# Turning by transposing transfers out of SBUF instead of on TensorE and through DRAM

## The chip, the cores and the metric

One core of one Trainium2 chip. The metric is the device time of one execution in microseconds (us). A profiled execution has a span, the time between its first and last instruction, and its own time, which is a little longer. Engine names are those of the profile: PE is TensorE's matmul, PEld its weight load, DVE VectorE, ACT ScalarE, POOL GpSimd, SP SyncE; SPq is SP's queue, on which nearly all transfers of this kernel are issued in order.

## What is computed

S = 2048 rows of D = 512 in bf16. A layer norm gives xn; a local attention (32 heads of 16, 8 keys at steps of 2 positions) and a mixing network both work on xn; the result is x + s * silu(g).

```python
def _B_ref(x, w1, w2, w3, w4):          # x is xn
    h = _gelu(_layernorm(x, axis=-1) @ w1)
    # g0..g3: the four quarters of h, moved along the rows by +1, -1, +2, -2
    hs = jnp.concatenate([g0, g1, g2, g3], axis=-1) @ w2
    x1 = x + hs
    h2 = _gelu(_layernorm(x1, axis=-1) @ w3) @ w4
    return x1 + h2

xn = _layernorm(A_x, axis=-1)
s = _A_ref(xn, A_wqkv, A_wo)            # q, k, v, softmax over 8 keys, @ wo
g = _silu(_B_ref(xn, B_w1, B_w2, B_w3, B_w4))
return A_x + s * g
```

w1 and w2 are 512x512, w3 is 512x1376, w4 1376x512, wqkv 512x1536.

## The kernel before

The rows are split by parity: p = 0 holds the even ones, p = 1 the odd ones, 1024 each. Each half is two chunks of 512 rows (chunk c has p = c // 2), each chunk four tiles of 128 rows. A tile of xn has rows on the partitions; a matmul that contracts over D needs D on the partitions, so each tile must be turned into "columns".

Every instruction that matters is pinned to the order in which the program emits it, engine by engine. So lines 505 to 599 are the order of the work, written out by hand: each engine, and SP's queue, takes its own instructions in this order. PE's sequence before the attention stage is: v, q and k of chunk 0, w1 of chunk 0, and then by chunk q, k, v, w1 with the turning work in between, then w2(0), q and k of chunk 3, w2(1), w2(2), w3(0), w2(3), w3(1) to w3(3). The attention stage (lines 878 to 936) follows from about 112 us; it mixes scores, softmax, values, w4 and the output projection.

What the steps below speak of:

- `Norm` (210 to 240): statistics and apply on DVE, the root on POOL (`rsqrt_eps`, 203). Layer norm l1 is applied in place on x (L237), l3 on x1 into a tile xn3.
- `turn` (296): 8 PE transposes (L302) of two tiles into PSUM and a DVE copy (L303) into xnT. It runs twice for each of chunks 1, 2 and 3; chunk 0 has `turn_one` and one `turn`.
- Row factors: the second norm in front of w1 works on rows that are normed already, so it is one factor for each row, `rows2` (248), made on POOL into r2b with rows on partitions. The product `scaled` (288, L291 on DVE) needs it along the free dimension on all partitions. `rows2_spread` (264, chunks 1 and 2) transposes r2b on PE (L266), copies it on DVE (L268), writes 4 rows of 128 to DRAM (L269) and reads them back broadcast to 128 partitions (L271). `rows2_here` (273, chunks 0 and 3) makes it with one DVE product (L277), one matmul with ones (L282) and a copy.
- `proj` (323) holds the matmuls of q, k and w1 (L328): 16 matmuls of 128x512 for a call with two output tiles, in a pair of PSUM banks. There are three such pairs, used in turn; ACT empties them (L339 q, L354 k, L400 w1's gelu).
- `w2` (415): 16 matmuls (L427), then on DVE the sum into x (L435), the statistics (L221), and the root on POOL.
- `columns` (443): the apply of l3, a write of the chunk to DRAM (L446), and a transposing transfer of 512x512 back into x1nT (L450), which `w3` (459, L469) reads.
- Loads on SP's queue: w3's is issued at line 545, behind the row factors of chunk 1; w4's at 574 and 578; `v_keep` (367, L377) writes v to DRAM.

Of the kernel before, what the change touches and what calls it, by code (L numbers as in the profile page):

```python
# [8 lines left out]
AF = mybir.ActivationFunctionType  # L9
ALU = mybir.AluOpType  # L10
BF16 = mybir.dt.bfloat16
# [9 lines left out]
def kernel(  # L21
# [17 lines left out]
    PE, DVE, ACT, POOL, SP = nc.tensor, nc.vector, nc.scalar, nc.gpsimd, nc.sync  # L39

    def pin(ins):

        return tc.keep_in_program_order(ins)

    P = 128
    S = 2048
    D = 512
    F = 1376
    ND = D // P
# [4 lines left out]
    CH = 512  # L54
    NCH = S // CH
    TPC = CH // P
# [22 lines left out]
    dram = ctx.enter_context(tc.tile_pool(name="dram", bufs=1, space=bass.MemoryType.DRAM))  # L79
# [16 lines left out]
    def single():  # L96
        cnt["s"] += 1
        return PS[:, 6 + (cnt["s"] - 1) % 2, :]


    xn = [b8([P, M // P, D], f"xn{p}") for p in range(2)]
# [24 lines left out]
    w3_sb = wpl.tile([P, WS], BF16, name="w3_sb", tag="w")[:, 0 : ND * F].rearrange("p (dt f) -> p dt f", f=F)  # L126
# [4 lines left out]
    ident = const.tile([P, P], BF16, name="ident")  # L131
# [61 lines left out]
    xnT = [b8([P, ND, M], f"xnT{p}") for p in range(2)]  # L193
# [2 lines left out]
    kM = [kbp.tile([P, ND, MK, 2], BF16, name=f"kM{p}", tag="kM") for p in range(2)]  # L196
    v_d = [dram.tile([MK, 2, D], BF16, name=f"v_d{p}") for p in range(2)]
    r2_d = dram.tile([NCH, CH], BF16, name="r2_d")
    x1n_dram = dram.tile([S, D], BF16, name="x1n_dram")
    vst = [b4([P, 2, 2, D], f"vst{i}") for i in range(2)]  # L200


# [4 lines left out]
    def small_t(name, shape, dt=F32):  # L207
        return small.tile(shape, dt, name=name, tag=name)
# [33 lines left out]
    def x_of(c):  # L242
        p, k = c // 2, c % 2
        return xn[p][:, k * TPC : (k + 1) * TPC, :]

    xn2Ts, r2s = {}, {}

    def rows2(c, ln):

        r2 = small_t("r2", [P, TPC])  # L250
        r2b = small_t("r2b", [P, TPC], BF16)
        eng = DVE if c == 0 else POOL
        pin(eng.tensor_tensor(out=r2, in0=ln.rstd, in1=ln.rstd, op=ALU.mult))
        pin(eng.tensor_tensor(out=r2, in0=r2, in1=ln.mv[:, :, 1], op=ALU.mult))
        if c == 0:
            pin(ACT.activation(r2, r2, AF.Sqrt, bias=eps_t[:]))
            with nc.allow_low_precision("bf16 row factors"):
                pin(DVE.reciprocal(out=r2b, in_=r2))
        else:
            rsqrt_eps(r2, r2)  # L260
            pin(POOL.tensor_copy(out=r2b, in_=r2))
        r2s[c] = r2b

    def rows2_spread(c):
        pt = single().bitcast(BF16)[0:TPC, 0:P]
        pin(PE.transpose(pt, r2s[c], ident[:]))  # L266
        t = small_t("r2t", [TPC, P], BF16)
        pin(DVE.tensor_copy(out=t, in_=pt))  # L268
        pin(SP.dma_start(out=r2_d[c].rearrange("(j q) -> j q", q=P), in_=t))  # L269
        xn2Ts[c] = b4([P, ND, CH], "xn2T")  # L270
        pin(SP.dma_start(out=xn2Ts[c][:, ND - 1, :], in_=r2_d[c : c + 1, :].to_broadcast([P, CH])))  # L271

    def rows2_here(c):

        xn2Ts[c] = t = b4([P, ND, CH], "xn2T")
        d = t[:, 0, :].rearrange("p (j q) -> p j q", q=P)
        pin(DVE.tensor_tensor(  # L277
            out=d, in0=ident.unsqueeze(1).to_broadcast([P, TPC, P]), in1=r2s[c].unsqueeze(2).to_broadcast([P, TPC, P]),
            op=ALU.mult,
        ))  # L280
        pt = single()
        pin(PE.matmul(pt, lhsT=ones_bf[:], rhs=t[:, 0, :], start=True, stop=True))  # L282
        if c == 0:
            pin(ACT.activation(t[:, ND - 1, :], pt, AF.Copy))
        else:
            pin(DVE.tensor_copy(out=t[:, ND - 1, :], in_=pt))

    def scaled(c):
        p, k = c // 2, c % 2
        t = xn2Ts[c]  # L290
        pin(DVE.tensor_tensor(  # L291
            out=t, in0=xnT[p][:, :, k * CH : (k + 1) * CH],
            in1=t[:, ND - 1, :].unsqueeze(1).to_broadcast([P, ND, CH]), op=ALU.mult,
        ))

    def turn(c, h):
        p, k = c // 2, c % 2
        i = k * TPC + 2 * h
        pt = single().bitcast(BF16).rearrange("p (a j q) -> p a j q", a=ND, j=2)
        for j in range(2):  # L300
            for dt in range(ND):
                pin(PE.transpose(pt[:, dt, j, :], xn[p][:, i + j, dt * P : (dt + 1) * P], ident[:]))  # L302
        pin(DVE.tensor_copy(  # L303
            out=xnT[p][:, :, i * P : (i + 2) * P], in_=pt.rearrange("p a j q -> p a (j q)")
        ))

    def turn_one(c, t):
        p, k = c // 2, c % 2
        i = k * TPC + t
        pt = single().bitcast(BF16)[:, 0 : ND * P].rearrange("p (a q) -> p a q", a=ND)  # L310
        for dt in range(ND):
            pin(PE.transpose(pt[:, dt, :], xn[p][:, i, dt * P : (dt + 1) * P], ident[:]))
        pin(ACT.activation(xnT[p][:, :, i * P : (i + 1) * P], pt, AF.Copy))

    def q_half(pts, lo, hi, nts=range(ND)):
        for nt in nts:
# [32 lines left out]
    def k_all(c, parts=(0, 1)):  # L349
        p, k = c // 2, c % 2  # L350
        for a in parts:
            pt = proj(c, a, wqk_sb[:, :, D : 2 * D], chunk(xnT, c))
            for e in range(2):
                pin(ACT.activation(  # L354
                    kM[p][:, 2 * a : 2 * a + 2, 8 + k * CH : 8 + (k + 1) * CH, e], pt, AF.Copy, scale=em[:, e : e + 1]
                ))
# [29 lines left out]
    def v_pair(p, t):  # L386
        pt = pair()
        for i in range(2):
            v_mm(p, t + i, pt[:, i, :])
        v_keep(p, t, 2, pt[:, 0, :])  # L390

    def v_pad(p):
        rows = v_d[p].rearrange("r e d -> (r e) d")
        pin(SP.dma_start(out=rows[0:16], in_=zero[0:16, :]))
        pin(SP.dma_start(out=rows[2 * (M + 8) : 2 * MK], in_=zero[0:4, :]))

    def w1(c, a):
        p, k = c // 2, c % 2
        pt = proj(c, a, w1_sb, xn2Ts[c])
        pin(ACT.activation(  # L400
            hT[p][:, 2 * a : 2 * a + 2, 1 + k * CH : 1 + (k + 1) * CH], pt, AF.Gelu_apprx_tanh
        ))
# [12 lines left out]
    def w2(c, order="a0 s0 a1 s1"):  # L415

        p, k = c // 2, c % 2
        x_c = x_of(c)
        ln = ln2[c] = Norm(x_c, b4([P, TPC, D], "xn3"), TPC, "l3")
        pts = []  # L420
        for h in range(TPC // 2):
            pt = pair()
            pts.append(pt)
            for j in range(2):
                m0 = k * CH + (2 * h + j) * P
                for g in range(ND):
                    pin(PE.matmul(  # L427
                        pt[:, j, :], lhsT=w2_src(p, g, m0), rhs=w2_sb[:, g, :],
                        start=(g == 0), stop=(g == ND - 1),
                    ))  # L430
        for what, i in (w for w in order.split()):
            if what == "a":
                h = int(i)
                xs = x_c[:, 2 * h : 2 * h + 2, :]
                pin(DVE.tensor_tensor(out=xs, in0=pts[h], in1=xs, op=ALU.add))  # L435
            elif what == "s":
                h = int(i)
                ln.stats(2 * h, 2 * h + 2)
            else:
                columns(c - 1)  # L440
        ln.root()

    def columns(c):
        ln = ln2[c]
        ln.apply(0, TPC)
        pin(SP.dma_start(  # L446
            out=x1n_dram[c * CH : (c + 1) * CH, :].rearrange("(i q) d -> q i d", q=P), in_=ln.dst
        ))
        x1nT = b4([P, ND, CH], "x1nT")
        pin(SP.dma_start_transpose(out=x1nT, in_=x1n_dram[c * CH : (c + 1) * CH, :]))  # L450
        x1nTs[c] = x1nT

    h3a, h3b = {}, {}
# [75 lines left out]
    for a in range(2):  # L529
# [10 lines left out]
    v_pair(0, 2)  # L540
    k_all(0, (1,))
    v_pad(0)
    w1(0, 0)
    rows2_spread(1)
    pin(SP.dma_start(out=w3_sb, in_=B_w3.rearrange("(dt q) f -> q dt f", q=P)))
    turn(1, 0)
    turn(1, 1)
    w1(0, 1)
    l2 = Norm(x_of(2), x_of(2), TPC, "l1")
    l2.stats(0, 4)  # L550
    l2.root()
    l2.apply(0, 4)
    rows2(2, l2)
    l3 = Norm(x_of(3), x_of(3), TPC, "l1")
    l3.stats(0, 4)
    l3.root()
    scaled(1)
    q_all(1)
    k_all(1)
    v_pair(0, 4)  # L560
    l3.apply(0, 4)
    rows2(3, l3)
    v_pair(0, 6)
    rows2_spread(2)
    w1(1, 0)
    turn(2, 0)
    turn(2, 1)
    w1(1, 1)
    scaled(2)
    q_all(2)  # L570
    turn(3, 0)
    turn(3, 1)
    k_all(2)
    pin(SP.dma_start(
        out=w4_sb[:, 0 : NF - 1, :],
        in_=B_w4[0 : (NF - 1) * P, :].rearrange("(ft q) n -> q ft n", q=P),
    ))
    pin(SP.dma_start(out=w4_sb[0:FL, NF - 1, :], in_=B_w4[(NF - 1) * P : F, :]))
    rows2_here(3)
    scaled(3)  # L580
    w1(2, 0)
    w1(2, 1)
    w1(3, 0)
    w1(3, 1)
    w2(0)
    columns(0)
    v_pad(1)
    q_all(3)
# [289 lines left out]
    for n in range(NU):  # L878
        now["n"] = n
        q = W4 * (n + 1) // NU - given  # L880
# [111 lines left out]
```

## Time and profile before

| | us |
|---|---|
| median of 3 runs | 197.82 (197.75 to 199.02) |
| profiled execution, own time | 197.26 |
| its span | 195.5 |
| PE busy | 185.5 |
| ACT busy | 133.3 |
| DVE busy | 117.8 |
| POOL busy | 19.1 |
| w2(0) begins on PE | 53.0 |
| w3(0) begins on PE | 70.8 |
| attention stage begins on PE | 112.2 |

The granted clock of TensorE was 0.996 of full speed. Busy times overlap: an engine that is busy for less than the span may still hold up another one at a single place, so what counts is which engine the others wait for at that place. A row of the time line is: start, length, engine, line of the kernel, operation, what it writes and reads, how many, and in brackets how long the engine was idle before and what ended that. For a transfer the row on SPq is its issue alone; the data land later.

### The profile page before, as it was taken

What the parts mean: (1) busy time and instruction counts of PE and PEld (TensorE: products, weight loads), DVE (VectorE), ACT (ScalarE), POOL (GpSimd) and SP (SyncE); (2) the same over time, 40 slices, a digit from 0 to 9 for tenths busy, and PEclk for the clock granted to TensorE, in tenths of its full rate; (3) what the DMA queues carried; (4) which work ended last, traced back from release to release, by engine and by line L of the source; (5) the groups of instructions that cost most, each with busy time, mean ns of one, the idle gap of its engine ahead of it and who ended that gap; (6) DMA issues with size and microseconds to landing.
All of it is one profiled execution on the core that took longest, in us unless ns stands there. A gap on an engine that the chain in (4) does not pass through costs nothing.

```text
span 195.5 us, 5255 instructions
## 1 busy us (share of the span) xinstructions
PE 185.5 (95%) x2253; PEld 91.8 (47%) x2283; DVE 117.8 (60%) x229; ACT 133.3 (68%) x151; POOL 19.1 (10%) x57
## 2 busy tenths in 40 slices
PE   7899999999999999999999999999999999999990
PEld 2474544554444444444444444445444544554540
DVE  5785767236076697494200035556487888798894
ACT  7399769649817615435656588877887876887871
POOL 3006066100002022006000000000000000000000
PEclk9999999999999999999999999999999999999998
DMA  4997480654000433752480051457565556582523
GB/s 131 339 368 239 132 282 15 218 158 157 0 0 3 136 83 109 215 107 65 110 260 0 0 162 60 157 166 232 153 216 161 137 155 215 127 247 51 171 91 126
DMA packets 33576, 28.12 MB, mean 144 GB/s; under 512 B 10760, under 2 KB 32528, under 8 KB 33552
## 3 DMA queue, kind: packets, MB, share of 16 engines
q1 hardware_dynamic: 33408, 27.71, 47.2%
q8 instruction: 18, 0.29, 0.6%
q10 hardware_dynamic: 144, 0.07, 0.1%
q14 instruction: 6, 0.05, 0.1%
HBM read 17.01 MB, written 8.67 MB: 131 GB/s over the span
## 4 chain that ended last, share of the span: by engine, by line
PE 85%; DMA 5%; DVE 4%; issue 2%; SPq 1%; ACT 1%
PE PS L469 19%; PE PS L328 19%; PE PS L764 19%; PE PS L427 5%; PE PS L811 4%; PE PS L795 4%; PE PS L652 3%; DMA wqk_sb<-in_A_wqkv_dram 3%; PE PS L626 3%; PE PS L362 3%; DMA x1nT<-x1n_dram 2%; PE PS L318 2%; PE PS L662 2%; PE PS L302 2%; DVE sg L825 2%
## 5 line engine op out<-in xcount | busy, mean ns | idle before, releaser
L469 PE MATMUL PS<-x1nT,w_sb 128*128 128x512 bf16 (+1 forms) x173 | 38.2, 379 | 0.4 <-DMA x1nT<-x1n_dram 0.3
L633 ACT ACTIVATE prob<-PS 128x1824 bf16<-128x1824 f32 x18 | 30.4, 1688 | 4.4 <-PE PS L626 3.6
L764 PE MATMUL PS<-w_sb,h3a 128*128 128x512 bf16 x112 | 29.2, 379 | 1.9 <-issue 1.7
L475 ACT ACTIVATE h3a<-PS 128x1024 bf16<-128x1024 f32 x16 | 16.4, 1024 | 21.0 <-PE PS L469 19.1
L777 DVE TENSOR_TENSOR xn<-PS,xn 128x512 bf16<-128x512 f32 x15 | 10.3, 686 | 32.0 <-PE PS L764 31.8
L469 PEld LDWEIGHTS <-w_sb 128*128 128x128 bf16 (+1 forms) x176 | 17.5, 100 | 20.9 <-issue 0.7
L328 PE MATMUL PS<-xnT,wqk_sb 128*128 128x512 bf16 x109 | 25.0, 379 | 0.2
L354 ACT ACTIVATE kM<-PS,em 128x1024 bf16<-128x1024 f32 x16 | 20.8, 1404 | 3.2 <-PE PS L328 3.2
L638 DVE TENSOR_TENSOR prob<-prob,maskb 128x1824 bf16<-128x1824 bf16 x18 | 19.8, 1102 | 1.8 <-ACT prob L633 1.8
L764 PEld LDWEIGHTS <-h3a 128*128 128x128 bf16 x128 | 11.3, 97 | 13.4 <-issue 1.2
L328 PEld LDWEIGHTS <-wqk_sb 128*128 128x128 bf16 x112 | 10.9, 98 | 12.8
L435 DVE TENSOR_TENSOR xn<-PS,xn 128x1024 bf16<-128x1024 f32 x8 | 9.6, 1213 | 11.3 <-PE PS L427 11.3
L811 PE MATMUL PS<-wo_sb,oT 128*128 128x512 bf16 (+1 forms) x68 | 15.5, 366 | 0.0
L328 PE MATMUL PS<-xn2T,w_sb 128*128 128x512 bf16 x62 | 14.6, 379 | 0.1
L427 PE MATMUL PS<-w_sb,hT 128*128 128x512 bf16 x63 | 14.4, 379 | 0.1
L821 ACT ACTIVATE sg<-PS 128x512 bf16<-128x512 f32 (+1 forms) x17 | 9.6, 572 | 6.1 <-PE PS L811 6.1
L764 PE MATMUL PS<-w_sb,h3b 128*128 128x512 bf16 (+1 forms) x44 | 12.8, 380 | 0.8 <-issue 0.8
L339 ACT ACTIVATE qT<-PS 128x1024 bf16<-128x1024 f32 x8 | 8.1, 1024 | 7.6 <-PE PS L328 7.6
L373 ACT ACTIVATE vst<-PS 128x512 bf16<-128x512 f32 (+1 forms) x12 | 8.8, 743 | 3.5 <-ACT sig L784 2.3
L221 DVE BATCH_NORM_STATS2 l1s<-xn 128x6 f32<-128x512 bf16 x16 | 10.1, 680 | 1.6 <-DMA xn<-in_A_x_dram 1.6
L400 ACT ACTIVATE hT<-PS 128x1024 bf16<-128x1024 f32 x8 | 8.1, 1031 | 3.8 <-PE PS L328 3.8
L221 DVE BATCH_NORM_STATS2 l3s<-xn 128x6 f32<-128x512 bf16 x16 | 10.2, 682 | 0.2
(105 smaller groups left out, 229.2 us busy)
## 6 DMA issues: line engine op xcount, KB each, us to landing
ring<-v_d SPq DMA_DIRECT2D x18, 256.0 KB, 3.3
v_d<-vst SPq DMA_DIRECT2D x16, 256.0 KB, 2.7
x1n_dram<-xn SPq DMA_DIRECT2D x4, 512.0 KB
xo<-in_A_x_dram SPq DMA_DIRECT2D x8, 256.0 KB, 4.1
ring<-rec_d SPq DMA_DIRECT2D x4, 456.0 KB, 4.7
out_dram<-xo SPq DMA_DIRECT2D x7, 256.0 KB
xn<-in_A_x_dram SPq DMA_DIRECT2D x6, 256.0 KB, 7.9
w_sb<-in_B_w_dram SPq DMA_DIRECT2D x1, 1376.0 KB
```

What stands on the lines that cost most here:

```text
L221: pin(DVE.bn_stats(out=self.st[:, j, :], in_=self.src[:, j, :]))
L328: pin(PE.matmul(pt[:, b, :], lhsT=w[:, dt, nt * P : (nt + 1) * P], rhs=rhs[:, dt, :], start=(dt == 0), stop=(dt == ND - 1),))
L354: pin(ACT.activation(kM[p][:, 2 * a : 2 * a + 2, 8 + k * CH : 8 + (k + 1) * CH, e], pt, AF.Copy, scale=em[:, e : e + 1]))
L427: pin(PE.matmul(pt[:, j, :], lhsT=w2_src(p, g, m0), rhs=w2_sb[:, g, :], start=(g == 0), stop=(g == ND - 1),))
L435: pin(DVE.tensor_tensor(out=xs, in0=pts[h], in1=xs, op=ALU.add))
L469: pin(PE.matmul(pt[:fs, ft % 2, :], lhsT=w3_sb[:, dt, ft * P : ft * P + fs], rhs=x1nT[:, dt, :], start=(dt == 0), stop=(dt == ND - 1),))
L475: pin(ACT.activation(t[:, o : o + 2, :], pt, AF.Gelu_apprx_tanh))
L633: pin(ACT.activation(pr, S_ps[:, :, 0 : ND * NQ], AF.Exp, scale=SCALE))
L638: pin(DVE.tensor_tensor(out=f, in0=f, in1=maskb[:], op=ALU.min))
L764: pin(PE.matmul(pt, lhsT=h3_of(c, ft)[:fs, jj * P : (jj + 1) * P], rhs=w4_sb[:fs, ft, :], start=(ft == 0), stop=(ft == NF - 1 and silu < 2),))
L777: pin(DVE.tensor_tensor(out=x_i, in0=pt, in1=x_i, op=ALU.add))
L811: pin(PE.matmul(pt[:, 0:W], lhsT=oT[p][:, dt, i * P : (i + 1) * P], rhs=wo["sb"][:, dt, c], start=(dt == 0), stop=(dt == ND - 1),))
```

## The change

Five things.

1. Chunks 2 and 3 are turned by four transposing transfers each, SBUF to SBUF, one for each tile of 128 rows (`turn_dma`), issued on SP's queue as soon as each tile is normed; the PE transposes and DVE copies of these chunks go. Chunk 1 is still turned on PE.
2. The row factors of chunks 1, 2 and 3 are written from r2b to DRAM as they are, in elements of 2 bytes, 128 x 4 (`rows2_write`), and read back broadcast at a later place (`rows2_read`). The PE transpose, the DVE copy and, for chunk 3, `rows2_here` go.
3. `columns` has four transposing transfers out of the normed tile xn3 in place of a write to DRAM and one transposing transfer out of it.
4. w2(0) stands ahead of the second call of w1 for chunk 3.
5. w3's load moves on SP's queue from behind the row factors of chunk 1 to behind those of chunk 3; the apply of chunk 3's l1 stands ahead of v's tiles 4 to 7 in the program, and `scaled(3)` directly behind k of chunk 2.

Per instruction on SP's queue between the w2 load and the w4 load, the new order is: v (2), v's zeros (2), write of factors 1, read 1, four transposing transfers of chunk 2, write 2, four of chunk 3, read 2, write 3, v (4), read 3, w3, w4.

```diff
-    x1n_dram = dram.tile([S, D], BF16, name="x1n_dram")
...
-    def rows2_spread(c):
-        pt = single().bitcast(BF16)[0:TPC, 0:P]
-        pin(PE.transpose(pt, r2s[c], ident[:]))
-        t = small_t("r2t", [TPC, P], BF16)
-        pin(DVE.tensor_copy(out=t, in_=pt))
-        pin(SP.dma_start(out=r2_d[c].rearrange("(j q) -> j q", q=P), in_=t))
+    def rows2_write(c):
+        pin(SP.dma_start(out=r2_d[c].rearrange("(j q) -> q j", q=P), in_=r2s[c]))
+
+    def rows2_read(c):
         xn2Ts[c] = b4([P, ND, CH], "xn2T")
         pin(SP.dma_start(out=xn2Ts[c][:, ND - 1, :], in_=r2_d[c : c + 1, :].to_broadcast([P, CH])))
...
+    def turn_dma(c):
+        p, k = c // 2, c % 2
+        for t in range(TPC):
+            i = k * TPC + t
+            pin(SP.dma_start_transpose(out=xnT[p][:, :, i * P : (i + 1) * P], in_=xn[p][:, i, :]))
...
     def columns(c):
         ln = ln2[c]
         ln.apply(0, TPC)
-        pin(SP.dma_start(
-            out=x1n_dram[c * CH : (c + 1) * CH, :].rearrange("(i q) d -> q i d", q=P), in_=ln.dst
-        ))
         x1nT = b4([P, ND, CH], "x1nT")
-        pin(SP.dma_start_transpose(out=x1nT, in_=x1n_dram[c * CH : (c + 1) * CH, :]))
+        for t in range(TPC):
+            pin(SP.dma_start_transpose(out=x1nT[:, :, t * P : (t + 1) * P], in_=ln.dst[:, t, :]))
...
     v_pad(0)
+    rows2_write(1)
     w1(0, 0)
-    rows2_spread(1)
-    pin(SP.dma_start(out=w3_sb, in_=B_w3.rearrange("(dt q) f -> q dt f", q=P)))
     turn(1, 0)
     turn(1, 1)
+    rows2_read(1)
     w1(0, 1)
...
     l2.apply(0, 4)
+    turn_dma(2)
     rows2(2, l2)
+    rows2_write(2)
...
     k_all(1)
+    l3.apply(0, 4)
+    turn_dma(3)
+    rows2_read(2)
+    rows2(3, l3)
+    rows2_write(3)
     v_pair(0, 4)
-    l3.apply(0, 4)
-    rows2(3, l3)
     v_pair(0, 6)
-    rows2_spread(2)
+    rows2_read(3)
+    pin(SP.dma_start(out=w3_sb, in_=B_w3.rearrange("(dt q) f -> q dt f", q=P)))
     w1(1, 0)
-    turn(2, 0)
-    turn(2, 1)
     w1(1, 1)
     scaled(2)
     q_all(2)
-    turn(3, 0)
-    turn(3, 1)
     k_all(2)
+    scaled(3)
...
-    rows2_here(3)
-    scaled(3)
     w1(2, 0)
     w1(2, 1)
     w1(3, 0)
+    w2(0)
     w1(3, 1)
-    w2(0)
     columns(0)
```

More of the change, by code (lines that the diff above doesn't have):

```diff
@@ L282, in rows2_here @@
         pin(PE.matmul(pt, lhsT=ones_bf[:], rhs=t[:, 0, :], start=True, stop=True))
[L283 to L286, printed above, removed]
+        pin(ACT.activation(t[:, ND - 1, :], pt, AF.Copy))
     def scaled(c):
```

## The prediction

> **What bounds the kernel now.** I read the busy table first, then the chain of waits, then what TensorE (PE) itself waited for in the stretch that the change touches, then the time lines of PE, SP, VectorE (DVE) and ScalarE (ACT) there.
>
> ```profile
> PE 185.5 (95%) x2253; PEld 91.8 (47%) x2283; DVE 117.8 (60%) x229; ACT 133.3 (68%) x151; POOL 19.1 (10%) x57
> PE 85%; DMA 5%; DVE 4%; issue 2%; SPq 1%; ACT 1%
> ```
> PE is busy 95% of the span and is 85% of the chain. Between 8 and 112 us, where every edit lies, it waits for others only twice:
>
> ```profile
> PE PS L318 <- DMA wqk_sb<-in_A_wqkv_dram: 0.3, 1, 0.3
> PE PS L469 <- DMA x1nT<-x1n_dram: 0.3, 1, 0.3
> ```
> So a PE instruction taken out there shortens the kernel by its length as long as no new wait appears. The "DMA x1nT" piece of 4.51 us in the chain is no gap: PE works through it, and w3 of chunk 0 waits 0.3 us at its end. These are the PE pieces that go (a row is start, length, what):
>
> ```profile
> 20.25 0.15 PE PS L266
> 33.48 0.15 PE PS L266
> 35.46 0.89 PE PS L302 x16
> 41.54 0.89 PE PS L302 x16
> 45.88 0.22 PE PS L282
> ```
> What takes their place runs on SP's queue, so its rows set the price:
>
> ```profile
> 37.01 0.47 SPq L269 DMA_DIRECT2D r_d<-r2t  x1
> 39.26 0.34 SPq L271 DMA_DIRECT2D xn2T<-r_d  x1
> 63.17 0.39 SPq L446 DMA_DIRECT2D x1n_dram<-xn  x1
> 66.16 2.20 SPq L450 DMA_TRANSPOSE x1nT<-x1n_dram  x1
> 77.81 2.03 SPq L450 DMA_TRANSPOSE x1nT<-x1n_dram  x1
> 83.37 1.93 SPq L450 DMA_TRANSPOSE x1nT<-x1n_dram  x1
> 94.87 1.31 SPq L450 DMA_TRANSPOSE x1nT<-x1n_dram  x1
> ```
> A transposing transfer holds SP for 1.31 to 2.20 us (median 1.98) for 512x512 out of DRAM; its first reader starts 2.44 us after the first issue ends (68.36 to 70.80). None out of SBUF is shown. The instructions that release and use the new transfers:
>
> ```profile
> 26.41 1.38 DVE L237 TENSOR_SCALAR xn<-xn,l1m,l1r 128x512 bf16<-128x512 bf16 x4 [1.48 <-POOL l1r L205]
> 32.81 1.38 DVE L237 TENSOR_SCALAR xn<-xn,l1m,l1r 128x512 bf16<-128x512 bf16 x4 [1.25 <-POOL l1r L205]
> 42.37 1.23 DVE L291 TENSOR_TENSOR xn2T<-xnT,xn2T 128x2048 bf16<-128x2048 bf16 x1 [5.13 <-DMA xn2T<-r_d]
> 44.20 5.17 ACT L354 ACTIVATE kM<-PS,em 128x1024 bf16<-128x1024 f32 x4 [1.60 <-PE PS L328]
> ```
>
> **The change, part by part.** Removed from PE: the two transposes of row factors (2 x 0.15), 32 turning transposes (2 x 0.89) and the one-matmul spread of chunk 3 (0.22): 2.30 us, all on the path. DVE loses four turning copies, two r2t copies, one diagonal product and one cast; it is 60% busy and waits there, so I count nothing. The order of the rest on DVE and POOL stays: the apply of chunk 3 stood behind the product of chunk 1 before too, and row factors 2 and 3 leave POOL at 28.6 and 35.0, before SP reaches their writes.
>
> PE in the new order, all from before's starts less what is gone ahead: q of chunk 2 starts at 36.9 (36.36 + 1.73 - 0.15 - 0.15 - 0.89), w1 of chunk 2 at 43.8 (46.10 - 2.30), w1 of chunk 3 at 47.25, w2(0) at 49.0, w3(0) at 68.2 (70.53, where it was ready, - 2.30).
>
> The turning transfers. Call SP's time for one of 128x512 t. By its elements against L450 it is a quarter, 0.33 to 0.55; by the instruction it is up to 2.20. I take 0.82: a fixed part of 0.43 (about the plain issues, 0.34 to 0.47) and a quarter of the other 1.55; L450, the same operation, is the nearest row. Both ends stay for the range. Four of chunk 2 start with the first piece of its apply, 26.6; they end at 29.9 and land at 32.3, needed at 36.9: 4.6 us of cover. The write of row factors 2 ends by 30.4. Four of chunk 3 start at 33.2, end at 36.5, land at 38.9; needed at 47.25.
>
> In front of the reads. SP works in order, so the read of row factors 2 now stands behind all eight turning transfers: issued at 36.5. Before, 3.1 us passed from that issue (39.26) to its product (42.37), and the product takes 1.23: ready at 40.85, needed at 43.8. This is the thinnest cover, 2.95 us. In general the issue is at max(33.2, 27.05 + 4t) + 4t and must be no later than 39.4, which holds up to t = 1.55; over it PE waits. Write 3 ends at 37.3, four v_d writes (2.52, the row at 34.40) at 39.8, read 3 is issued then, its product is ready at 44.2, needed at 47.25. The products stand in order on DVE; behind them is only the sum of w2(0), after 50.7.
>
> The element writes (128 x 4 values of 2 bytes, 512 pieces): the nearest issue is L269, 0.24 to 0.47, and L446, which also has 512 pieces, 0.39; I take 0.45. Landing: read 39.26 came 1.78 after L269's issue; 128 pieces of rec_d keep their reader at most 2.1 us. I take 4 us (estimate: 2.1 and as much again for four times the pieces) and bounds 1 to 8.4 (four times 2.1). Write 1 goes at 21.1, lands by 25.6, read 1 serves at 28.7 a product that DVE reaches at 30.2. SP is free at 26.0, before 26.6.
>
> [...]
>
> w3's load goes behind read 3, from 22.88 to about 40.2, w4's two behind it. The one of 1376 KB at 39.65 kept the DMA engines busy to about 46, so w3 is in at 46 and w4 at 52; needed at 68.2 and 110. Without that cover it would be its 6 us.
>
> w2(0) ahead of the last quarter of w1: 1.73 earlier for chunk 0, nothing of PE's sum. Its first sum to the first applied piece took 62.1 - 53.03 = 9.1 us; now 58.1. Four transfers in place of a write (63.17), a wait and L450 (66.16): issued by 61.4, landed at 63.8, needed at 68.2. The 0.27 us that w3(0) waited goes. Chunks 1 to 3: the first piece of chunk 1 at 70.6, landed 76.4, needed at 81.3; 2 and 3 have more. The v_d zeros and x loads behind them are needed after 96.
>
> Late next: ACT. Four L354 take 5.17 and PE gives them three groups of 1.73; with the spread of 0.22 gone, the spare 0.18 before w1 of chunk 3 (49.55 against 49.37) is used up, and likewise the 0.13 at 33.63. I charge 0.1 for both.
>
> Sum: 2.30 + 0.27 - 0.10 = 2.47. The profiled execution took 197.26 (span 195.5 and 1.76 around it): 194.8. The median of the runs shown is 0.56 above it, 197.82: 195.35, predicted as 195.3.
>
> **The rivals.**
>
> A transfer out of SBUF costs SP a whole L450 or more. For it: the four L450 differ by 0.9 with one size, so the cost is not elements alone. Against: the smallest, 1.31, is already under the bound. At t = 1.98 read 2 leaves at 42.9, 3.5 late, w3(0) waits 0.3 more: 197.82 + 3.8 - 2.47 = 199.1, less than 1% slower. At 2.20: 5.25 and 1.15 late, 201.8. It breaks even at about 1.85 and is over 1% slower from 2.1.
>
> A part of it: t between 1.55 and 2.1 eats the gain: 195.9 to 199.8.
>
> The transfers are priced by 128x128 block, serially. A 512x512 has 16 blocks and lands within 4.64 us of its issue, 0.29 a block; with 1.31, the least L450, charged to each of a transfer's four blocks, t = 5.24, read 2 leaves at 69.0, 29.6 late, and w3 of the four chunks then waits about 13, 8, 11 and 11: some 268. [...]
>
> Element writes landing after more than 5.6 us hold read 3 past 42.9, after more than 7.4 also read 1 past 28.95. At 9 us: 1.6 and 1.8 late, 198.8.
>
> ACT's releases of PSUM swallow half of the gain: 196.6. PE waited for none of them before, so it is unlikely.
>
> **How the numbers follow.** Forecast 0.56, the middle band of t 0.11, t of 2.1 or more 0.22, by block 0.04, element writes 0.04, half the gain 0.03. About 1% is what a measurement of this kernel can tell from no change: under 195.84 is faster, over 199.80 slower. Faster 0.55 (the forecast less its edge); slower 0.30 (0.22, 0.04 and most of the element case); same 0.15. The forecast's own range is 194.5 to 195.9; the whole reaches to 202.0, just past t = 2.20, and leaves out the block case and the dearer half of 2.1 and more.
>
> **What would show it.** Right: PE without those five pieces and with no wait for xnT, xn2T or x1nT; four transposing issues on SP within 6.2 us; w1 of chunk 2 near 43.8; w3(0) near 68.2. Wrong: PE waiting at q of chunk 2 (transfers), at w1 of chunk 2 (read 2 behind them), at w1 of chunk 3 (element writes) or at w3 (transfers of x1nT), or L354 releasing PE.

## The result and the profile after

The changed kernel took 240.14 us (median of 4 runs, 238.85 to 241.8) against 197.78 for the kernel before (4 runs, 197.31 to 199.02): 1.216 times as long, 95% interval 1.211 to 1.221. The profiled execution took 238.85, with a span of 237.1; the span before was 195.5. So 41.6 us are to be explained. Ratios and intervals, here and below, leave out runs more than 1.5% above the fastest of the same kernel.

First the page of the kernel after, with the lines that answer to the first two shown of before (busy time by engine; share of the chain by engine), and two more: the clock that TensorE was granted in 40 slices, and the lines of the chain.

```profile
PE 190.5 (80%) x2218; PEld 91.7 (39%) x2248; DVE 113.6 (48%) x221; ACT 133.5 (56%) x151; POOL 18.2 (8%) x57
...
PEclk9999996598575557999999999999999999999998
...
PE 59%; DMA 25%; ACT 5%; DVE 4%; SPq 4%; issue 3%; DVEq 0%
DMA r_d<-r2b 23%; PE PS L467 16%; PE PS L763 16%; PE PS L328 5%; PE PS L427 4%; ACT kM L354 3%; PE PS L810 3%; PE PS L794 3%; PE PS L651 3%; PE PS L625 2%; SPq L313 2%; DMA xn2T<-r_d 2%; PE PS L141 2%; PE PS L661 2%; PE PS L318 2%
```

One transfer, the element write of the row factors (r_d from r2b), now holds 23% of the chain, about 54 us; before, no transfer held more than 3%. PE is busy 5.0 us *longer*, though 2.30 us of its work are gone, and the clock line stands at 5 to 8 tenths in nine of the ten slices from the 7th on. The waits of PE (what, us in total, times, longest):

```profile
PE PS L328 <- DVE xn2T L285: 35.8, 3, 19.3
...
PE PS L651 <- issue: 0.9, 1, 0.9
PE PS L661 <- issue: 0.5, 1, 0.5
```

All 35.8 us are w1 of chunks 1, 2 and 3 waiting for the product of columns and row factors. What the product waits for (waits of DVE):

```profile
DVE xn2T L285 <- DMA xn2T<-r_d: 53.1, 3, 24.4
```

And the cause is on SP's queue (start, length, line, what):

```profile
21.39 0.39 SPq L264 DMA_DIRECT2D r_d<-r2b  x1
35.81 0.34 SPq L268 DMA_DIRECT2D xn2T<-r_d  x1
36.25 5.22 SPq L313 DMA_TRANSPOSE xnT<-xn  x4
41.56 0.53 SPq L264 DMA_DIRECT2D r_d<-r2b  x1
42.19 5.12 SPq L313 DMA_TRANSPOSE xnT<-xn  x4
57.87 0.33 SPq L268 DMA_DIRECT2D xn2T<-r_d  x1
58.30 1.13 SPq L264 DMA_DIRECT2D r_d<-r2b  x1
59.52 2.55 SPq L377 DMA_DIRECT2D v_d<-vst  x4
81.83 0.34 SPq L268 DMA_DIRECT2D xn2T<-r_d  x1
```

L264 is the element write, L268 the read that needs its data. From the end of write 1 (21.78) to read 1 (35.81) SP stands for 14.0 us with nothing in between. From write 2 to read 2 it is 15.8 us, of which the transposing transfers of chunk 3 use 5.1; from write 3 to read 3, 22.4 us, of which four v writes use 2.6. And SP works in order: while read 1 waits, the four turning transfers of chunk 2, whose tiles DVE had normed by 27.0 (25.62 and 1.38), wait too, to 36.25, and so does everything behind them. DVE hands the wait on as well. In its own order the apply of chunk 3 stands behind the product of chunk 1, so it ran at 41.59, where before it ran at 32.81, and the transfers of chunk 3 need it:

```profile
40.45 1.23 DVE L285 TENSOR_TENSOR xn2T<-xnT,xn2T 128x2048 bf16<-128x2048 bf16 x1 [10.78 <-DMA xn2T<-r_d]
41.59 1.37 DVE L236 TENSOR_SCALAR xn<-xn,l1m,l1r 128x512 bf16<-128x512 bf16 x4
```

The rows of PE (in brackets the idle time before):

```profile
41.73 6.32 PE L328 MATMUL PS<-xn2T,w_sb 128*128 128x512 bf16 x16 [9.03 <-DVE xn2T L285]
...
62.22 6.32 PE L328 MATMUL PS<-xn2T,w_sb 128*128 128x512 bf16 x16 [7.48 <-DVE xn2T L285]
...
87.84 3.59 PE L328 MATMUL PS<-xn2T,w_sb 128*128 128x512 bf16 x8 [19.30 <-DVE xn2T L285]
```

Each wait is paid twice: behind it 16 matmuls take 6.32 us and 8 take 3.59. In the kernel before, matmuls of this size took 3.62 and 1.89:

```profile
36.19 1.89 PE L328 MATMUL PS<-xn2T,w_sb 128*128 128x512 bf16 x8
...
42.27 3.62 PE L328 MATMUL PS<-xnT,wqk_sb 128*128 128x512 bf16 x16
```

The table of stretches of the kernel after (stretch, length, busy time of PE, PEld, DVE, ACT and POOL with counts, granted clock, share of the DMA engines, GB/s) shows why:

```profile
38.00:46.00 8.00, 4.27 (x11) 1.52 (x12) 2.52 (x5) 0.64 (x1) 0.00 (x0) 0.50 0.73 114
46.00:58.00 12.00, 8.74 (x38) 3.75 (x37) 0.00 (x0) 8.20 (x8) 0.00 (x0) 0.93 1.29 23
58.00:65.00 7.00, 2.78 (x7) 1.04 (x8) 1.23 (x1) 0.40 (x1) 0.00 (x0) 0.50 1.13 78
```

The clock granted in the two stretches with a wait and the matmuls behind it is 0.50, and 0.93 in the one between them; behind the third wait it is 0.50 from 87.84 to 91.20. That makes 2.7 + 2.7 + 1.7 = 7.1 us more of PE work. The waits ahead of these matmuls were 9.0, 7.5 and 19.3 us. The kernels further down show shorter ones: 8 matmuls behind a wait of 1.3 us took 1.90 us and 16 behind 2.1 took 3.63, about as in before (1.89 and 3.62); 8 behind 4.8 took 3.23 and 8 behind 5.1 took 3.59, these last at a granted clock of 0.50.

The account: 35.8 (waits) + 7.1 (half clock) - 2.3 (work removed) - 0.6 (two waits of 0.3 before that are gone) + 1.8 (attention stage: from the last w3 matmul to the end 84.9 us, before 83.1) = 41.8, against 41.6 measured. w3(0) begins at 110.6 (before 70.8), so nearly all of it lies ahead of it.

### The profile page after: what moved, and what is told of

It is laid out like the page before. It is cut to its first block, busy times and chain, and to the rows that moved or that the text cites. A ratio compares the mean times of both kernels' runs of the same rounds, so it can differ in the third digit from the quotient of the medians.

```text
span 237.1 us, 5228 instructions
## 1 busy us (share of the span) xinstructions
PE 190.5 (80%) x2218; PEld 91.7 (39%) x2248; DVE 113.6 (48%) x221; ACT 133.5 (56%) x151; POOL 18.2 (8%) x57
## 4 chain that ended last, share of the span: by engine, by line
PE 59%; DMA 25%; ACT 5%; DVE 4%; SPq 4%; issue 3%; DVEq 0%
DMA r_d<-r2b 23%; PE PS L467 16%; PE PS L763 16%; PE PS L328 5%; PE PS L427 4%; ACT kM L354 3%; PE PS L810 3%; PE PS L794 3%; PE PS L651 3%; PE PS L625 2%; SPq L313 2%; DMA xn2T<-r_d 2%; PE PS L141 2%; PE PS L661 2%; PE PS L318 2%
## 5 line engine op out<-in xcount | busy, mean ns | idle before, releaser
L328 PE MATMUL PS<-xn2T,w_sb 128*128 128x512 bf16 x63 | 21.9, 514 | 35.9 <-DVE xn2T L285 35.8
L285 DVE TENSOR_TENSOR xn2T<-xnT,xn2T 128x2048 bf16<-128x2048 bf16 x4 | 4.9, 1217 | 53.1 <-DMA xn2T<-r_d 53.1
L328 PEld LDWEIGHTS <-w_sb 128*128 128x128 bf16 x64 | 7.6, 124 | 48.7 <-DVE xn2T L285 37.1
L427 PE MATMUL PS<-w_sb,hT 128*128 128x512 bf16 x63 | 14.6, 382 | 0.1
```

The lines of the kernel that those rows point to most:

```text
L328: pin(PE.matmul(pt[:, b, :], lhsT=w[:, dt, nt * P : (nt + 1) * P], rhs=rhs[:, dt, :], start=(dt == 0), stop=(dt == ND - 1),))
L427: pin(PE.matmul(pt[:, j, :], lhsT=w2_src(p, g, m0), rhs=w2_sb[:, g, :], start=(g == 0), stop=(g == ND - 1),))
```

## The experiments

The theory: an element write is slow in itself, SP in order hands its slowness to everything behind, and the turning transfers are innocent. The rivals: the transfers of the neighbourhood slow it down; the transposing transfers hold the reads back; the moved loads do.

**Writes alone.** In this kernel the whole computation is left out; each write of small pieces is followed on SP by a read of what it wrote, and nothing else runs. The output is a copy of x. The lines shown are three of the forms: 512 pieces of 2 B side by side, 128 of 8 B, and 512 of 2 B that lie 512 B apart.

```diff
+    pin(SP.dma_start(out=d1.rearrange("(j q) -> q j", q=P), in_=src1))
+    pin(SP.dma_start(out=s1, in_=d1.unsqueeze(0).to_broadcast([P, CH])))
...
+    pin(SP.dma_start(out=d5.rearrange("(q j) -> q j", q=P), in_=src5))
...
+    pin(SP.dma_start(out=d6.rearrange("(j q) w -> q j w", q=P)[:, :, 0:1], in_=src6.unsqueeze(2)))
```

> This kernel leaves out the whole computation: it only writes small row vectors to DRAM in several forms and reads each back, one after another, each write after the read before has landed; x is copied to the output at the end. What is looked at is how long SP waits between the end of a write's issue and the issue of its read. Theory A (one DMA engine takes its pieces one after another, about 0.44 us each, from 14.0 us for 512 pieces on 16 engines): 512 pieces of 2 bytes 14 us both times, 256 pieces 7, 128 pieces of 2 bytes 3.5 to 4, 128 pieces of 8 bytes the same 3.5 to 4, 512 pieces each in a block of its own 14, 512 pieces of 4 bytes 14, the four rows of before 1 to 2. Rival B (the write is slow because of the transposing transfers and loads around it): 512 pieces land within 4 us here. Rival C (pieces that fall into the same block of DRAM collide): 512 pieces apart land in under 5 us, 512 side by side in 14. Rival D (2 bytes are the trouble): 512 pieces of 4 bytes in under 5.

SP's waits between the end of a write's issue and the read of its data (in this order: 128 pieces of 2 B, 512 of 2 B, 512 of 4 B, 128 of 8 B, 512 of 2 B that lie 512 B apart):

```profile
SPq L90 <- DMA d_128x<-src: 17.8, 1, 17.8
SPq L75 <- DMA d_512x<-src: 14.2, 1, 14.2
...
SPq L105 <- DMA d_512x<-src: 8.5, 1, 8.5
...
SPq L95 <- DMA d_128x<-src: 3.7, 1, 3.7
...
SPq L100 <- DMA d_apart<-src: 1.3, 1, 1.3
```

The element write takes 14.2 us with nothing around it, so the neighbourhood is not needed, though it may add to it (15.8 and 22.4 us for writes 2 and 3 above). And it is not the number of pieces: 512 of them, 512 bytes apart, take 1.3; side by side, 256 took 14.0 and 128 took 17.8. What is left is where they land. The write of before, 4 rows of 256 B, took 0.8. A transposing transfer of 128x128 held SP for 1.21 us, one of 128x512 for 1.24: at these two sizes the price is for the transfer, not for its blocks.

**Distance alone.** The computation is left out again; 512 elements of 2 B are written at distances of 2 to 512 bytes. The lines shown are those of 16 bytes; the others differ in the width alone.

```diff
+    d8, s8 = dr("d_pitch16", [CH, 8]), sink("s_pitch16", (P, TPC))
...
+    pin(SP.dma_start(out=d8.rearrange("(j q) w -> q j w", q=P)[:, :, 0:1], in_=src8.unsqueeze(2)))
```

> Leaves out the whole computation: 512 pieces of 2 bytes are written to DRAM at growing distances (2, 4, 8, 16, 32, 64, 128, 256, 512 bytes from piece to piece) and a few of them read back, one write after another; x is copied to the output. What is looked at is how long SP waits between each write's issue and its read. From the forms before: 14.2 us for 512 side by side and for 256 side by side, 17.8 for 128, 3.8 for 128 of 8 bytes, 8.6 for 512 of 4 bytes, 1.4 for 512 that are 512 bytes apart. So pieces in one block go one after another (theory C), and theory A (one engine's pieces one after another) has fallen. By C the wait is in proportion to the pieces in a block: with a block of 64 bytes it halves with each doubling of the distance, 14, 7, 3.5, 2 and reaches 1.4 at 64 bytes; with a block of 256 bytes it halves to 256; with a block of 512 it would still be near 2 or more at 256.

SP's waits again; L75 is a distance of 2 B, L80 4, L85 8, L90 16, L95 32, L100 64, L105 128:

```profile
SPq L75 <- DMA d_pitch<-src: 14.6, 1, 14.6
SPq L80 <- DMA d_pitch<-src: 8.5, 1, 8.5
...
SPq L85 <- DMA d_pitch<-src: 4.2, 1, 4.2
...
SPq L90 <- DMA d_pitch<-src: 2.5, 1, 2.5
...
SPq L95 <- DMA d_pitch<-src: 1.7, 1, 1.7
SPq L100 <- DMA d_pitch<-src: 1.6, 1, 1.6
SPq L105 <- DMA d_pitch<-src: 1.5, 1, 1.5
```

The time above a floor of 1.3 us falls to about a half or less with each doubling of the distance and is almost gone from 32 to 64 bytes on. Counted by the pieces that lie within 64 bytes, 32 take 13.3 us over the floor, some 0.42 each, and 16, 8 and 4 pieces give 0.45, 0.36 and 0.30. That such pieces wait for each other, and that it ends near 64 bytes, is the author's estimate from these times; no trace shows it. The 128 pieces in one row that took 17.8 do not fit this count, and stay unexplained.

**The element writes alone, on the kernel before** (chunks 1 and 2; no transposing transfer out of SBUF, no moved load).

```diff
-    rows2_spread(1)
+    rows2_write(1)
+    rows2_read(1)
...
-    rows2_spread(2)
+    rows2_write(2)
+    rows2_read(2)
```

> The kernel before with only the row factors of chunks 1 and 2 written in elements of 2 bytes, at the places of the old writes. Theory A: read 1 leaves SP 14 us after the write, near 35.5, w1 of chunk 1 starts some 7 to 8 us late, PE then runs for some us at half clock, and the second write comes later still: 207 to 218. Rival B: under 201, as there is no transposing transfer out of SBUF next to the writes.

223.84 us in one run (the profiled one; span 222.1), 26 more than before. PE's waits:

```profile
PE PS L289 <- DVE xn2T L284: 13.1, 1, 13.1
PE PS L335 <- DVE xn2T L298: 9.1, 1, 9.1
```

SP stands from 21.1 to 34.9 and from 41.2 to 61.2. The second, 20.0 us beside v's writes and w3's load, is 5.8 longer than the 14.2 alone, and the expectation was missed upward by as much. In the change itself write 3 took 22.4 with v's writes alone beside it, so these may be enough to add to it. Two of the three element writes give 26 of the 42 us, without any transposing transfer.

**The change without the element writes** (factors as before).

```diff
-    rows2_write(1)
     w1(0, 0)
+    rows2_spread(1)
...
-    rows2_write(2)
-    rows2_read(2)
-    rows2_write(3)
-    rows2_read(3)
+    rows2_spread(2)
...
-    scaled(3)
+    rows2_here(3)
+    scaled(3)
```

> The changed kernel with the row factors made as in the kernel before (PE transpose, copy, a write of four rows; chunk 3 by a matmul). Theory A (the element writes alone are the loss): the transposing transfers keep the gain forecast for them: 1.78 us of PE transposes and 0.27 us of wait go, less 0.1, so about 195.9 against 197.8, and PE waits for no transfer. Rival B (the transposing transfers at 1.2 us each on SP, or their landing, cost much themselves): over 205.

205.87 us, 1.040 times before (1.034 to 1.046): 34 us better than the change, but not the gain that was expected. The rows of SP around the read of chunk 2 (L277):

```profile
26.37 11.51 SPq L325 DMA_TRANSPOSE xnT<-xn  x8
37.98 3.59 SPq L389 DMA_DIRECT2D v_d<-vst  x4
41.66 0.47 SPq L275 DMA_DIRECT2D r_d<-r2t  x1
43.73 0.36 SPq L277 DMA_DIRECT2D xn2T<-r_d  x1
```

All eight turning transfers and four v writes now stand ahead of write 2; the product comes at 48.76, PE waits 7.0 us and then runs at a granted clock of 0.50 until 53 us. This order is not that of the change, where write 2 stood ahead of the transfers of chunk 3; but it shows that the order on SP costs by itself, with the cheap writes too.

**128 pieces of 8 bytes, and w3's load, and the order of read 3.** Three kernels on the change. The first writes four factors of a partition side by side (and so in another order than the product needs: its time alone is read); the second has w3's load at its old place besides; the third is the first with v's writes behind read 3.

```diff
-        pin(SP.dma_start(out=r2_d[c].rearrange("(j q) -> q j", q=P), in_=r2s[c]))
+        pin(SP.dma_start(out=r2_d[c].rearrange("(q j) -> q j", q=P), in_=r2s[c]))
...
     rows2_read(1)
+    pin(SP.dma_start(out=w3_sb, in_=B_w3.rearrange("(dt q) f -> q dt f", q=P)))
...
-    v_pair(0, 4)
-    v_pair(0, 6)
+    v_late = []
+    v_pair(0, 4, v_late)
+    v_pair(0, 6, v_late)
     rows2_read(3)
+    for put in v_late:
+        put()
```

> The changed kernel with the row factors written as 128 pieces of 8 bytes in place of 512 of 2, one piece for each partition; the factors then stand in another order, so the rows are scaled by each other's factors. Theory A: 8 pieces for an engine land in about 4 us, and everything else stands as forecast: 195.3 to 196.5. Rival B: still over 220, since the transfers around it are unchanged. Rival C (pieces in the same block collide): in between, since four times fewer pieces still lie side by side: 200 to 215.

> The kernel of 128 pieces of 8 bytes (row factors in another order) with w3's load back at its old place, behind read 1. There, read 3 was issued at 44.5 and its product began at 51.8, 7.3 us later, where the kernel before needed 3.1, and PE waited 5.1 us for it. Theory L (w3's load issued right behind read 3 slows its landing): with w4 behind it instead, as in the kernel before, the landing is back at 3 to 4 us, PE waits 2 us at most, total 198 to 200. Theory V (the four v writes ahead of it, 1 MB, slow it): landing still 6 to 7 us, total 202 to 204.

> The kernel of 128 pieces of 8 bytes (row factors in another order) with the four v writes moved behind read 3, so that neither they nor the loads stand directly ahead of it and w3's load follows 2.5 us or more later. Write 3 leaves at 39.6 and lands by 43.6, so read 3 at 43.6. Theories L and V alike: landing in 3 to 4 us, product ready at 48.5, PE waits 0.5 us or less: 196 to 198. If its landing stays at 7 us for another reason: 201 or more.

| kernel | us | against before | PE waits at w1 | read 3 to product 3 |
|---|---|---|---|---|
| 8-byte pieces | 203.5 | 1.030 (1.024 to 1.035) | 5.1 | 44.49 to 51.77 |
| and w3 early | 204.17 (one run) | | 2.1 + 4.8 | 47.03 to 52.48 |
| and read 3 first | 197.65 | 1.000 (0.997 to 1.003) | 1.3 | 42.88 to 47.05 |

With 8 pieces to 64 bytes in place of 32, write 1 takes 2.8 us in place of 14.0, and the time goes from 240.1 to 203.5: the form of this write alone is worth 36.6 us. (In the third kernel write 3, behind the transposing transfers, took 4.0.) The time lies in the range of the rival that pieces collide, but what is left of the loss is read 3. It was expected to serve its product 3.1 us after its issue, as in before; directly behind v's writes, and with w3's and w4's loads directly behind it, it took 7.3. With w3's load moved away it took 5.5, and the time did not fall: so at most a part of the delay is that load's. With v's writes behind read 3, and so the loads further back too, it took 4.2. How much belongs to v's writes and how much to the loads is not separated. w3's load in its old place costs elsewhere: beside it the four transposing transfers take 7.68 us in place of 5.23 (26.24 to 33.92).

In the third of these the w3 stage begins 1.5 us earlier than before, and the whole is no faster. The attention stage, which the change does not touch, takes 85.0 us in place of 83.1.

**Order mended, factors in the right order** (the read goes into a tile of its own, and the product reads it in steps of four elements).

```diff
-    turn_dma(2)
+    turn_dma(2, (0, 1))
     rows2(2, l2)
     rows2_write(2)
+    turn_dma(2, (2, 3))
+    rows2_read(2)
...
+                in1=r2w[c].rearrange("p (q j) -> p j q", j=TPC).unsqueeze(1).to_broadcast([P, ND, TPC, P]),
```

> All of it put right: factors written as 128 pieces of 8 bytes, read back in that order into a tile of their own and put in order by the step of the DVE product's operand (so the result is that of the reference); write 2 after two of the transposing transfers of chunk 2, read 2 ahead of those of chunk 3, write 3 after two of these, read 3 ahead of the v writes. Read 2 at 33.5 and read 3 at 40.5, products ready at 38 and 45.5 or, if the stepped operand doubles the product's time, 39.5 and 47. PE needs them at 43.8 and 47.25. So PE loses its 2.30 us and waits for nothing: 195.3 to 196.5. If the transposing transfers cost something that is not on SP: 198 or more.

198.01 us (median of 10 runs, 195.43 to 199.32), ratio 0.996 (0.991 to 1.000): about even, and not the gain that was expected. The profiled execution took 199.32, and PE waits 2.1 us in it for wqk at its start. The stepped operand takes the product from 1.23 to 2.29 us, PE waits 1.0 at w1 of chunk 3, and the attention stage again takes 85.0. Read 3 left at 44.53, not at 40.5: 2.1 us of that is the late start, and two of the transposing transfers of chunk 3 held SP for 4.95 us together, where the other two took 2.50; this stays open.

**Columns and w2(0) alone, on the kernel before.** The edits of parts 3 and 4 of the change and nothing else.

> The kernel before with two parts of the change alone: columns by four transposing transfers out of SBUF for each chunk, and w2(0) ahead of the second call of w1 for chunk 3. PE has as many instructions as before. Theory S (each such transfer holds SP for 1.2 us and lands 1.2 later, so chunk 0's last piece is there well before w3 needs it): w3(0) begins within 0.3 us of its place before (70.5 to 70.8 us from the start of the span), the attention stage takes the 83.3 us that it takes before, and the time is 197.3 to 197.9. Rival T (the transfers of chunks 1 to 3 meet the loads of x and w4 and come late): PE waits for x1nT by 1 us or more, 199 or more. Theory P (the issue waits of PE in the attention stage hang on the number of PE instructions ahead of it): none above 0.2 us here. Its rival (they come from the transposing transfers or from w2(0) standing earlier): waits of 0.5 to 1.1 us there, 198.3 to 199.2.

196.48 us, ratio 0.997 (0.994 to 1.000). The wait of w3 is gone, the attention stage takes 82.9, and there is no issue wait above 0.2 us in it. That is 0.8 us under the expected range. In the profiled execution w3(0) begins at 70.11 in place of 70.80: 0.3 is the wait that went, 0.2 lies at the start of the span, where before waited for wqk (first q at 8.94, here at 8.70), and 0.2 is left over. The interval just excludes no change.

**Reads between the turning transfers.** Parts 1, 3 and 4 and w3's load late; the factors as before, but chunk 2's made earlier, so that its write and read stand between the two groups of turning transfers. The lines are against the kernel before, and of this stretch alone.

```diff
     l2.apply(0, 4)
+    turn_dma(2)
...
     k_all(1)
+    rows2_spread(2)
+    l3.apply(0, 4)
+    turn_dma(3)
+    rows2(3, l3)
     v_pair(0, 4)
-    l3.apply(0, 4)
-    rows2(3, l3)
     v_pair(0, 6)
-    rows2_spread(2)
```

**The same with PE's start cut finer.** The ten matmuls on ones at the very start, which feed nothing, become 42 shorter ones of nearly the same columns in all: 32 PE instructions more, as many as the turning transposes that went.

```diff
-    for i in range(10):
+    for i in range(42):
         pin(PE.matmul(
-            PS[:, 6 + i % 2, :], lhsT=ones_bf[:], rhs=ones_bf.unsqueeze(1).to_broadcast([P, TPC, P]),
+            PS[:, 6 + i % 2, 0:122], lhsT=ones_bf[:], rhs=ones_bf[:, 0:122],
```

> The changed kernel without the element writes: the row factors are made as before, but the PE transpose of chunk 2's stands ahead of v's tiles 4 and 5, and so its write and its read stand between the four transposing transfers of chunk 2 and the four of chunk 3 on SP; v's writes and w3's load stand behind the latter. Theory S (what was left over after the element writes is SP's order alone): write 2 at about 31.5, read 2 at about 33.5, the product of chunk 2 by 38, w1 of chunk 2 at 44, no PE wait of more than 0.3 us between 10 and 110 us, the attention stage begins at 110.2. With the issue waits in the attention stage, as in every kernel so far with 32 or more PE instructions fewer (0.6 to 1.6 us): 195.9 to 197.0; without them 195.4. Rival T (the reads are late wherever transposing transfers stand near them, because the transfers slow each other down): PE waits 1 us or more at w1 of chunk 2 or 3, and 197.5 or more.

> The same kernel with PE's ten matmuls of 512 columns on ones at the very start, which feed nothing, cut into 42 of 122 columns: 32 PE instructions more, as many as the turning transposes that went, so that PE has as many as before. Theory P (the waits of PE for its own instructions in the attention stage hang on how many instructions stand ahead of it): the issue waits of 0.3 to 1.1 us are gone, the attention stage takes 83.3 us, and the time is 0.6 to 1.5 under the unpadded kernel: 194.8 to 195.6. Rival Q (they come from the transfers or from the changed times of the other engines): the waits and the time stay within 0.3 us of the unpadded kernel's.

Unpadded: 196.81 us, ratio 0.997 (0.995 to 1.000). SP in the new order:

```profile
26.27 5.21 SPq L318 DMA_TRANSPOSE xnT<-xn  x4
31.58 0.42 SPq L268 DMA_DIRECT2D r_d<-r2t  x1
32.93 0.36 SPq L270 DMA_DIRECT2D xn2T<-r_d  x1
33.35 5.13 SPq L318 DMA_TRANSPOSE xnT<-xn  x4
```

Product 2 comes at 36.39, between 10 and 110 us PE waits for nothing, and w3(0) begins at 68.0, 2.8 us earlier than before. Of these, 1.8 are the turning transposes and 0.3 the wait of w3, as forecast; 0.6 lie at the start of the span (first q at 8.37 in place of 8.94), which the edits do not touch and where the wait for wqk ran from 0 to 2.1 us over these profiles; 0.2 is left over. But the rows of PE in the attention stage have waits that no other engine ends:

```profile
142.40 0.24 PE L653 MATMUL PS<-prob,ring 128*32 128x57 bf16 x7 [1.10 <-issue]
...
157.79 0.32 PE L663 MATMUL PS<-prob,den_st 128*32 128x114 bf16 x9 [0.54 <-issue]
...
174.06 0.41 PE L653 MATMUL PS<-prob,ring 128*32 128x57 bf16 x31 [0.40 <-issue]
```

Padded: 194.71 us, ratio 0.985 (0.983 to 0.988): 1.5% under the kernel before, and its slowest run (194.95) is under the fastest of the unpadded kernel (196.34). These waits are gone, and the attention stage takes 82.8 us in place of 85.4, as the theory of the PE instructions ahead forecast (its time 0.1 us below the expected range).

**Half of the padding:** 26 matmuls of 198 columns, 16 instructions more.

> The kernel of read2_between again, with half of the padding: the ten matmuls on ones at the start, which feed nothing, cut into 26 of 198 columns, 16 PE instructions more and 16 fewer than before. Theory N (what counts is how many instructions fewer there are than in the kernel before): PE's waits for its own instructions in the attention stage shrink to about half of 2.0 us, and the time lies between the two kernels, 195.3 to 196.2. Rival M (what counts is where the stage's instructions fall in the stream, so that the waits come back at other places with any shift that is not the one of before): waits of 1 to 2 us, at other lines or other tiles than at 142.40 and 157.79, 196.0 to 197.0. Third (any padding ahead is enough): no wait above 0.2 us, 194.5 to 195.2.

196.03 us, ratio 0.991 (0.987 to 0.995), stage 84.5, one wait left:

```profile
157.67 0.25 PE L653 MATMUL PS<-prob,ring 128*32 128x57 bf16 x9 [0.77 <-issue]
```

The time lies between the two, but in the ranges of the first theory and of its rival alike (they meet at 196.0 to 196.2), so it does not decide; and the one wait of 0.77 is not all of the 1.7 us by which the stage is longer than the padded one's. A count of weight loads tells more. In the change itself, in the 8-byte kernel with read 3 first and in the one with the reads between, the first wait comes after 1237 weight loads and the second after 1619 or 1620; here too the one that is left comes after 1620. The change reaches the first of these places at 184.79 us and the kernel with the reads between at 142.40, with other transfers around it. So these waits have a fixed place in PE's stream rather than in time, and a shift of the code moves other matmuls there. Where they occur, short ones stand there (128x57, 128x114). That alone is not enough: in the kernel before, the 1237th load falls among short matmuls too, without a wait, and near the 1620th 32 of them take 0.72 us in place of 0.42. The distance is 383 loads, 766 instructions with their matmuls. What makes PE wait at these places is not shown.

## Why the prediction was wrong

The step that failed is the landing of the element writes: "I take 4 us ... and bounds 1 to 8.4 (four times 2.1)". Measured: 14.0 from write 1 to read 1, with the queue empty in between, and 14.2 alone. A late landing was among the rivals ("Element writes landing after more than 5.6 us hold read 3 past 42.9, after more than 7.4 also read 1 past 28.95"), with 198.8 us at 9 us and a chance of 0.04. That rival named the right wait; its size was far outside the bounds. The bound was scaled with the number of pieces, and the runs show that number not to matter: 512 pieces 512 B apart land in 1.3 us. The row it came from (rec_d, 28.5 KB in 128 pieces, so some 228 B each) said nothing about pieces of 2 B side by side.

The second failure is what a late read costs, and the size alone does not make up for it. The prediction looked at each read for itself, each from an unchanged time of its write. Put 14 us into its own sum and read 3 leaves at 37.3 + 14 = 51.3, 8.4 late: some 204 in all, not 240. On SP's queue the wait of read 1 held back the turning transfers of chunk 2, which held back write 2, and so on to the third, so that the three latencies added up: 9.0 + 7.5 + 19.3 us of PE's waits. DVE's order passed it on as well: the prediction noted that the apply of chunk 3 stands behind the product of chunk 1, and put no price on it.

Not in the prediction at all: that each such wait is followed by matmuls at a granted clock of 0.50 (7.1 us).

Point by point, the others:

- **The PE pieces that go (2.30 us): right.** With the clock whole, PE is busy 183.4 us in the kernel with read 3 first, against 185.5.
- **t, SP's time for one turning transfer: 0.82 forecast, 1.2 to 1.3 measured** (1196 to 1297 ns in the change), inside its bounds and under the 1.55 at which PE would wait. The split into a fixed part of 0.43 and a quarter of the rest was wrong: a 128x512 takes SP as long as a 128x128 (1.24 and 1.21), so the fixed part is nearly all. For the same reason the rival "by 128x128 block", priced at 268 us, falls. The rival "a whole L450" came near at its low end (1.31) and falls at the median (1.98). Beside w3's load four of them took 7.68, and in the kernel with the order mended two took 4.95.
- **Read 2 behind all eight transfers, "the thinnest cover, 2.95 us": it held, with less left.** With t at 1.2 its issue comes at 37.9 in the kernel with read 3 first, under the 39.4 allowed, and its product runs from 41.44 to 42.67, 0.7 us before PE starts w1 of chunk 2 at 43.39. With w3's load early the transfers stretch and PE waits 2.1; where write 2 also stands behind the transfers and v's writes, as in the kernel without element writes, PE waits 7.0. The 3.1 us from a read's issue to its product were 3.1 to 7.3 in these kernels.
- **w3's load late: right.** No PE wait for it; early it stretches the turning transfers. (The load at 39.65 that the prediction reads as 1376 KB is w4's, of 1280 KB; nothing hangs on it.)
- **w2(0) sooner and columns out of SBUF: right.** The wait of w3 goes. That w3(0) begins at 68.0 where 68.2 was forecast, in the kernel that does parts 1, 3 and 4 in a good order, is partly luck: that kernel keeps 0.52 us of PE work for the row factors that the forecast took out, and its first q came 0.57 earlier.
- **ACT's releases: right to leave small.** PE never waits for ACT there in any of these kernels.
- **The sum, 2.47: never measured as it stands.** The nearest is the padded kernel, 2.4 to 3.4 us (1.2 to 1.7%) under before. It keeps the 0.52 us for the row factors, so its share of the sum is 1.95; in the profile w3(0) begins 2.4 earlier, 0.2 of it at the start, and the attention stage is 0.3 shorter. A gain of this size is there, but only when the issue waits are taken away, which the sum did not know.

So most of the gain was there, and three things ate it: element writes side by side, worth 36.6 of the 42 us with all that follows from them; the order on SP; and 1.8 us more in the attention stage, of which 1.4 are the issue waits.

## What to carry to other kernels

In these runs a write of small pieces is priced by how close they lie in DRAM, up to some 64 bytes, and hardly by their number: 512 pieces took 14.6 us side by side and 1.6 at 64 bytes, and 256 side by side took 14.0. Have one engine turn the data first (a PE transpose of 0.15 us did it here), or keep the pieces far apart. A read that needs such a write, put on a queue that works in order, hands its wait to everything behind it (14.0, 15.8 and 22.4 us from write to read here, and 35.8 us of PE's waits), so put what does not depend on it ahead and count the latencies as a sum. And when PE instructions are taken out, look at the stages that the change does not touch for new waits with no releaser: here 32 more instructions at the start, for the same columns in all, gave 2.1 us back.

## What the runs showed that was not expected

- 512 elements of 2 bytes take 14.6, 8.5, 4.2, 2.5, 1.7 and 1.6 us to land at distances of 2, 4, 8, 16, 32 and 64 bytes. 128 elements in one row took 17.8, more than 512 did; this stays open.
- A transposing transfer within SBUF holds SP for 1.2 us, at 128x128 as at 128x512; beside the load of w3 four of them took 7.68 us in place of 5.23.
- PE waits 0.3 to 1.1 us for no other engine after the 1237th, 1620th and (once) 2002nd weight load, where matmuls of 57 or 114 columns stand there; with 32 instructions more ahead of them the waits are gone. Why is not settled.
- A product whose one operand is read in steps of four elements took 2.29 us in place of 1.23.
